# Top-k attention with a gated feed-forward layer: copies of near-limit columns by four tiles, and reciprocals transposed into another PSUM bank

## The chip, the cores and the metric

The kernel runs on one core of a Trainium2 chip. Its time is device microseconds of one execution; every kernel is run several times and the median counts. A profile is one further execution, recorded by the hardware profiler. Its engines are called by the names of the profile: PE is TensorE (matmuls; PEld are its weight loads), DVE is VectorE, ACT is ScalarE, POOL is GpSimd, SP is SyncE, which issues most DMAs here.

## The reference

For 8 batches, 8 heads, 576 rows and head width 64, attention keeps in each row the scores that are at least the row's 32nd largest, takes the softmax over them and multiplies by v. The heads side by side (512 columns) go through a feed-forward layer with a convolution of width 3 along the rows in its gate.

```python
scores = scale * np.matmul(q, k.transpose(0, 1, 3, 2))
kth = np.partition(scores, -32, axis=-1)[..., -32:-31]
scores = np.where(scores >= kth, scores, -1e9)
attn = np.exp(scores - np.max(scores, axis=-1, keepdims=True))
attn = attn / (np.sum(attn, axis=-1, keepdims=True) + 1e-09)
x = np.matmul(attn, v)                      # then heads side by side: (8, 576, 512)
h = np.maximum(x @ w_in, 0.0)               # 512 -> 1024
conv = conv_w[0] * h[s - 1] + conv_w[1] * h[s] + conv_w[2] * h[s + 1]
out = (h / (1.0 + np.exp(-conv))) @ w_out   # 1024 -> 512
```

## The kernel before

A tile is 128 rows of scores of one head (or the last 64 rows of both heads of a pair) by 576 columns; there are 288 tiles, 36 to a batch. A batch has two parts: first four pairs of heads with six tiles each, then the four pairs again with three tiles each, the last of which holds the 64 remaining rows of both heads (a "single" tile).

`iteration(it)` is a software pipeline written out by hand. In one iteration seven tiles are at work, each in another stage: TensorE computes the scores of tile it+3, ScalarE copies those of tile it+2 out of PSUM into one of eight row buffers (`rows`, 592 columns each, eight spare ones on either side of the 576 scores), VectorE takes the largest eight of each of seven chunks of tile it, and for tile it-1 the ranks near the 32nd out of these candidates (lines 281 to 288; the ranks are written into the spare columns of the tile's row buffer). For tile it-2 ScalarE computes signs against the estimated limit and counts them (`sides`), and GpSimd multiplies them in (`flip`). For tile it-3 ScalarE takes the exponential into a PSUM tile (`expo`, line 310). For tile it-4 VectorE finds the largest value below the limit (`below`), picks the limit (`select`, line 317) and multiplies mask and exponential with a running sum (`weigh`, line 331). For tile it-5 TensorE transposes the weights into bank `pt` (line 343) and ScalarE copies them out (`pT`, lines 348 and 351); with the tile's last head come the transposes of the 64 end columns into bank `mixed` (`tails`, line 356). One iteration later follows the product with v (line 375).

Within the loop the order of each engine's instructions is the order of this code for TensorE, ScalarE, VectorE and GpSimd; SyncE's and everything after the loop is ordered by a scheduler at build time. Matmuls of the feed-forward layer (lines 453 and 610) are put between the others by `run_units`, a fixed amount to an iteration as long as there are any ready.

Two steps beside this pipeline are touched by the change:

- `edges` keeps two spare columns of each tile (columns 6 and 7 of its row buffer, where the ranks next to the limit stand) for a count at the end of the kernel. It runs for eight tiles at once, on ScalarE (line 293), right behind the signs of the tile that fills the eighth row buffer. The first of the eight buffers is the next one that VectorE writes ranks into (line 285, the maximum of 56 candidates into columns 0 to 7), so that maximum waits for the copy.
- `norms` runs for each two pairs of heads, 32 times in all, in the iteration after VectorE has taken the reciprocals of the row sums (line 391). TensorE transposes the reciprocals (line 397), so far into bank `pt`, ScalarE copies them to SBUF (`rT`, line 399), and SyncE writes them to DRAM and reads them back spread over partitions (`rb`, lines 401 to 413), for GpSimd to multiply with (line 421).

The tiles `t_ps` and `e_ps` are parts of one PSUM tile, `weights_ps`, and so is `above`, which `select` reads. The bank `mixed` holds the end columns of the scores (columns 0 to 127), the transposed ends (128 to 255) and the product with v (256 to 511).

Of the kernel before, what the change touches and what calls it, by code (L numbers as in the profile page):

```python
# [29 lines left out]

XNB = 6
XBUFS = 8
EBUFS = 2
ZB = 3
SB = 2
# [33 lines left out]
def attend_and_feed(ctx: ExitStack, tc: tile.TileContext, q, k, v, weights, out, shared, finish=None):  # L69
    nc = tc.nc  # L70
    exact = finish is None
# [3 lines left out]
    ident, wi, wo, cw, cr, kth, edge = shared  # L75
# [31 lines left out]
    for i in range(10):  # L107
        nc.vector.memset(above[:, i:i + 1], float(S - 2 * (TOPK - (i + 1 if i < 8 else 0))))
    rows = const.tile([P, XBUFS, S + 16], F32, name="rows")
    sided = []  # L110
# [15 lines left out]
    def bank(name):  # L126
        return ps.tile([P, BANK], F32, name=name, tag=name, bufs=1)

    s_ps = [bank(f"s{h}") for h in range(2)]
# [113 lines left out]
    def evacuate(t):  # L243
        t.row = rows[:, t.n % XBUFS]
        x = t.x = t.row[:, 8:S + 8]
        at = TAIL if t.h else 0
        nc.scalar.copy(out=x[:, at:at + MAIN], in_=s_ps[t.h])  # L247
        if t.single:
            nc.scalar.copy(out=x[:, MAIN:S], in_=edge_ps[:, 0:TAIL])
        elif t.h == 0:  # L250
            r = t.n % XBUFS
            if r + 1 < XBUFS:
                first, step = r * (S + 16) + 8 + MAIN, S + 16 - MAIN
                ends = flat[:, first:first + 2 * step].rearrange("p (h c) -> p h c", h=2)[:, :, 0:TAIL]
                nc.scalar.copy(out=ends, in_=edge_ps.rearrange("p (h c) -> p h c", h=2))
            else:
                nc.scalar.copy(out=x[:, MAIN:S], in_=edge_ps[:, 0:TAIL])
                nc.scalar.copy(out=rows[:, 0, 8:8 + TAIL], in_=edge_ps[:, TAIL:2 * TAIL])
# [29 lines left out]
                    out=some, in_to_replace=m, in_values=some, imm_value=LOW)  # L288

    def edges(t):  # L290
        if t.n % XBUFS == XBUFS - 1 or t.n == NT - 1:
            n = t.n % XBUFS + 1
            nc.scalar.copy(out=edge[:, t.n + 1 - n:t.n + 1], in_=rows[:, 0:n, 6:8])  # L293

    def sides(t):
        t.cnt = att.tile([P, 1], F32, name="cnt", bufs=8)
        t.side = sided[t.n % SB]
        nc.scalar.activation(out=t.side[:, 2:S + 2], in_=t.x, func=AF.Sign, scale=-OVER, bias=t.row[:, 7:8],  # L298
                             accum_out=t.cnt)
# [6 lines left out]
    def expo(t):  # L306
        if t.h == 0:
            t.st.e2 = att.tile([P, 2 * S], F32, name="e2", bufs=EBUFS)
        t.e = t.st.e2[:, t.h * S:(t.h + 1) * S]
        nc.scalar.activation(out=e_ps, in_=t.x, func=AF.Exp, scale=scale, bias=t.shift)  # L310
# [79 lines left out]
        nc.vector.tensor_scalar(sums_ps[:, 0:n], pc.duo.sums[:, 0:n], 1e-9, None, ALU.add)  # L390
        nc.vector.reciprocal(rec[:, 0:n], sums_ps[:, 0:n])

    def norms(pc):
        n, w = pc.n, pc.c1 - pc.c0
        odd = pc.n % 2
        tp = bank("pt")
        nc.tensor.transpose(tp[0:2 * n, 0:P], pc.duo.rec[:, 0:2 * n], ident)
        rT = att.tile([SUMS, P], F32, name="rT", bufs=1)
        nc.scalar.copy(out=rT[0:2 * n], in_=tp[0:2 * n, 0:P])
        row = dram.tile([SUMS, P], F32, name="row", bufs=4)  # L400
        nc.sync.dma_start(out=row[0:2 * n], in_=rT[0:2 * n])
        rb = att.tile([P, 2, WIDE], F32, name="rb", bufs=1)
        for one in pc.duo.pcs:
            at = one.g % 2
            one.rb = rb[:, at, 0:w]
            for h in range(2):
                r = slice(h * D, (h + 1) * D)
                k, c = at * n + odd * lead // TAIL, odd * lead
                nc.sync.dma_start(out=rb[r, at, c:c + n // 2 * P].rearrange("d (i p) -> d i p", p=P),
                                  in_=row[k + h:k + n // 2 * 2:2, :].unsqueeze(0).broadcast_to([D, n // 2, P]))  # L410
                if odd:
                    k, c = (at * n, 0) if lead else (at * n + n - 1, w - TAIL)
                    nc.sync.dma_start(out=rb[r, at, c:c + TAIL],
                                      in_=row[k:k + 1, (1 - h) * TAIL:(2 - h) * TAIL].broadcast_to([D, TAIL]))
# [130 lines left out]
    class Contract:  # L545
# [11 lines left out]
        def split(self):  # L557
# [3 lines left out]
            if late and len(parts) == 1:  # L561
                for pool, name, n, size in ((att, "e2", EBUFS, 2 * S), (att, "pT", PTB, 2 * MAIN)):
                    for _ in range(n):
# [116 lines left out]
    pcs, work = [], []  # L680
    for b in range(B):
        for part, blocks in enumerate(PARTS):
            for g in range(NPAIR):
                pc = Box()
# [4 lines left out]
                for i in blocks:  # L689
# [4 lines left out]
                    for h in range(1 if single else 2):  # L694
                        t = Box()
# [5 lines left out]
    NT = len(work)  # L701
# [24 lines left out]
    def run_units(budget, only=None):  # L726
        while budget > 0.0 or (only is not None and only.cur is not None):
            for lane in lanes if only is None else (only,):
                if lane.cur is None:
                    lane.unit = lane.take()  # L730
                    if lane.unit is not None:
                        lane.cur, lane.left = lane.unit.pieces(), lane.unit.count
                if lane.cur is not None:
                    break
            else:
                return budget
            budget -= next(lane.cur)
            lane.left -= 1
            if lane.left == 0:
                next(lane.cur, None)  # L740
                lane.cur = None
                if lane.unit.final:
                    lane.finished.append(lane.unit)
        return budget
# [34 lines left out]
    av_next, out_next, rec_next, norm_wait, tail_next = [], [], [], [], []  # L779

    def iteration(it):
        nonlocal av_next, out_next, rec_next
        n = it + 3
        state.it = it
        pre, tA, tB, tC = (tiles.get(i) for i in (it + 2, it, it - 1, it - 2))
        tX, tD, tE = tiles.get(it - 3), tiles.get(it - 4), tiles.get(it - 5)
# [7 lines left out]
        crowded = n < NT and not work[n].single and work[n].h == 0  # L794
# [5 lines left out]
        if n < NT:  # L800
            t = tiles[n] = work[n]
            pc = t.pc
# [2 lines left out]

        if tC is not None and not exact:
            sides(tC)
            edges(tC)
        if pre is not None:
            evacuate(pre)  # L810
        if tE is not None:
# [31 lines left out]
        recs, rec_next = rec_next, []  # L843
# [6 lines left out]
        convert_act()  # L850
        if tX is not None:
            expo(tX)
        while tanh_now:
            e = tanh_now.popleft()
            e.tanh()
            if e.pooled():
                pool_tasks.append((it + 1, 2.01 * e.n / S + 0.1, e.gate_pool))
            else:
                gates.append(e)
# [3 lines left out]
        if norm_wait and norm_wait[0][0] <= it and not any(b < norm_wait[0][1].b - (norm_wait[0][1].g < XNB - NPAIR) for b in held):  # L863
            pc = norm_wait.pop(0)[1]
# [3 lines left out]
        feed = EARLY if state.blocks < BLOCKS else FEED if work[min(max(it, 0), NT - 1)].pc.part == 0 else LEAN  # L868
        state.credit = min(state.credit + (feed if it < NT + 5 else 9.0), PE_CAP)
        state.credit -= max(state.credit, 0.0) - run_units(max(state.credit, 0.0))  # L870
        for pc in recs:
            norms(pc)
        if both:
            tails(tE)
        if n + 1 < NT and not (work[n].single or work[n + 1].single or work[n + 1].h):
# [28 lines left out]
    with tc.manual_schedule(engines=engines) if engines else nullcontext():  # L904
        for pc in pcs[0:2]:
            fetch(pc)
        load_blocks(W_FIRST)
        for it in range(-3, NT + 6):
            iteration(it)
    if finish is not None:  # L910
        finish(edge_ps[0:1, 0:1])
    while expands or contracts or any(x.waiting for x in lanes) or pool_tasks or tanh_next or tanh_now or gates:
        it += 1
        iteration(it)
# [121 lines left out]
```

## Time and profile before

| | us |
|---|---|
| median of 3 runs (lowest, highest) | 1142.49 (1139.71, 1142.71) |
| profiled execution, its own time | 1140.73 |
| its span, first to last instruction | 1138.9 |
| first and last selection `weigh` (288 of them) | 28.0, 1068.5 |
| first and last of the 36 copies of line 293 | 47.8, 1063.2 |
| PE, DVE, ACT, POOL busy in the span | 1050.0, 1039.2, 988.1, 959.3 |

The loop over tiles takes nearly the whole span; until some 150 us the weights are converted beside it, and the last 70 us are the rest of the feed-forward layer. A busy time is the union of an engine's instructions as the profiler saw them. Matmuls are pipelined and their ends are modelled, so a busy PE need not be at its peak. A wait is an engine's idle time before an instruction, put down to the instruction of another engine that ended it; "issue" means that the profile shows no such instruction. Times in lists and rows are microseconds from the start of the span.

### The profile page before, as it was taken

The numbers are of one execution on the slowest core, as the hardware profiler recorded it, in microseconds if no ns is written. First come the engines' busy times: TensorE is split into PE (matmuls) and PEld (weight loads), VectorE is DVE, ScalarE is ACT, GpSimd is POOL, SyncE is SP. The second block draws the span as 40 slices with busy tenths as digits, with TensorE's granted clock in tenths as the row PEclk, the third lists the DMA queues.
The fourth block names the chain that finished last, engine by engine and source line by source line (L and its number), as shares of the span: only waits on it lengthen the run. The fifth ranks groups of instructions, "written<-read, shape, count | busy, mean of one in ns | idle before, by whom it ended". The sixth has DMA issues, their size and how long they took to land.

```text
span 1138.9 us, 27947 instructions
## 1 busy us (share of the span) xinstructions
PE 1050.0 (92%) x7970; PEld 769.6 (68%) x7970; DVE 1039.2 (91%) x5822; ACT 988.1 (87%) x2468; POOL 959.3 (84%) x1260
## 2 busy tenths in 40 slices
PE   5866689999999999999999999999899999999997
PEld 1443356676776767776777767776677767777785
DVE  6999999999899999999999999999999999999770
ACT  6999989898898888989999988989999888998651
POOL 5988978799898979899898979899898989899710
PEclk9988899999999999999999999999999999999999
DMA  7232221223221322223221222123222232132101
GB/s 254 85 102 79 78 85 55 61 79 107 70 79 51 109 87 73 63 75 127 60 79 62 95 86 87 53 87 117 67 61 82 70 111 87 50 90 71 32 25 50
DMA packets 71158, 92.28 MB, mean 81 GB/s; under 512 B 12848, under 2 KB 37712, under 8 KB 70992
## 3 DMA queue, kind: packets, MB, share of 16 engines
q1 hardware_dynamic: 70992, 90.38, 25.0%
q8 instruction: 66, 1.08, 0.4%
q14 instruction: 100, 0.82, 0.2%
HBM read 80.76 MB, written 9.58 MB: 79 GB/s over the span
## 4 chain that ended last, share of the span: by engine, by line
PE 59%; DVE 23%; ACT 14%; issue 2%; DMA 0%; POOL 0%; SPq 0%; ACTq 0%; DVEq 0%; POOLq 0%
PE mc L610 13%; PE me L453 12%; PE pt L343 9%; PE mixed L375 9%; PE s L241 7%; DVE cand L265 6%; DVE e L331 5%; DVE z L313 4%; ACT side L298 3%; ACT weights_ps L310 3%; PE mixed L378 2%; DVE cand L287 2%; PE mixed L224 2%; PE s L234 2%; PE weights_ps L610 1%
## 5 line engine op out<-in xcount | busy, mean ns | idle before, releaser
L265 DVE MAX8 cand<-rows 128x8 f32<-128x82 f32 (+1 forms) x2016 | 481.5, 240 | 0.0
L303 POOL TENSOR_TENSOR z<-rows,side 128x579 f32<-128x579 f32 x288 | 347.2, 1206 | 75.2 <-ACT side L298 74.1
L310 ACT ACTIVATE weights_ps<-rows,z 128x576 f32<-128x576 f32 x288 | 218.7, 760 | 26.5 <-DVE e L331 14.8
L331 DVE SCALAR_TENSOR_TENSOR e<-rows,kth,weights_ps 128x576 f32<-128x576 f32 x288 | 231.9, 805 | 0.9 <-PE mixed L356 0.7
L453 PE MATMUL me<-x_hi,wi 128*128 128x258 f32 (+1 forms) x952 | 229.6, 312 | 0.7 <-ACT g L467 0.7
L298 ACT ACTIVATE side<-rows 128x576 bf16<-128x576 f32 x288 | 222.3, 772 | 0.0
L313 DVE MAX8 z<-z 128x8 f32<-128x576 f32 x288 | 213.8, 742 | 0.0
L343 PEld LDWEIGHTS pt<-ident,e 128*128 128x128 f32 x1152 | 124.9, 144 | 125.9 <-issue 47.5
L610 PE MATMUL mc<-wo,split 128*128 128x512 f32 x732 | 197.4, 402 | 0.0
L343 PE MATMUL pt<-ident,e 128*128 128x128 f32 x1152 | 194.3, 293 | 3.0 <-DVE e L331 1.6
L351 ACT COPY pT<-pt 128x512 f32<-128x512 f32 x256 | 152.5, 596 | 44.2 <-PE pt L343 42.7
L241 PE MATMUL s<-k,q 64*128 64x512 f32 x512 | 180.7, 677 | 4.2 <-ACT rows L247 4.2
L247 ACT COPY rows<-s 128x512 f32<-128x512 f32 x288 | 166.6, 578 | 13.6 <-PE s L241 10.9
L375 PE MATMUL mixed<-pT,vn 128*64 128x128 f32 (+1 forms) x2560 | 168.1, 275 | 2.2 <-ACT pTt L361 2.2
L453 PEld LDWEIGHTS me<-x_hi,wi 128*128 128x128 f32 x952 | 162.7, 191 | 1.5 <-ACT g L467 1.4
L375 PEld LDWEIGHTS mixed<-pT,vn 128*64 128x64 f32 x2560 | 132.3, 141 | 24.3 <-issue 7.8
L610 PEld LDWEIGHTS mc<-wo,split 128*128 128x128 f32 x732 | 128.9, 189 | 20.9 <-POOL split L589 0.4
L453 PE MATMUL me<-x_lo,wi 128*128 128x258 f32 (+1 forms) x476 | 141.7, 298 | 0.0
L285 DVE MAX8 rows<-cand 128x8 f32<-128x21 f32 x576 | 105.9, 184 | 36.8 <-ACT edge L293 36.8
L486 POOL TENSOR_SCALAR t<-g,cr 128x256 f32<-128x256 f32 (+1 forms) x230 | 117.7, 512 | 0.0
L500 POOL TENSOR_TENSOR t<-t,t 128x256 f32<-128x256 f32 (+1 forms) x115 | 92.3, 803 | 9.6
L453 PEld LDWEIGHTS me<-x_lo,wi 128*128 128x128 f32 x476 | 90.9, 191 | 0.1
(133 smaller groups left out, 1778.1 us busy)
## 6 DMA issues: line engine op xcount, KB each, us to landing
k<-in_k_dram SPq DMA_DIRECT2D x64, 352.0 KB
q<-in_q_dram SPq DMA_DIRECT2D x64, 288.0 KB
vn<-in_v_main_dram SPq DMA_DIRECT2D x64, 256.0 KB
out_dram<-o SPq DMA_DIRECT2D x26, 256.0 KB
rb<-row SPq DMA_DIRECT2D x64, 96.0 KB
raw<-in_w_in_dram SPq DMA_DIRECT2D x16, 256.0 KB
vt<-in_v_tail_dram SPq DMA_DIRECT2D x64, 64.0 KB
raw<-in_w_out_dram SPq DMA_DIRECT2D x16, 256.0 KB
```

Of the source, the lines that this page charges most:

```text
L241: nc.tensor.matmul(s_ps[h], lhsT=qx[d, at], rhs=kx[d, h * TAIL:h * TAIL + MAIN], start=True, stop=True)
L247: nc.scalar.copy(out=x[:, at:at + MAIN], in_=s_ps[t.h])
L265: yield lambda c=c, at=at, n=n: nc.vector.max(out=t.cand[:, c:8 * CHUNKS:CHUNKS], in_=t.x[:, at:at + n])
L298: nc.scalar.activation(out=t.side[:, 2:S + 2], in_=t.x, func=AF.Sign, scale=-OVER, bias=t.row[:, 7:8], accum_out=t.cnt)
L303: nc.gpsimd.tensor_tensor(t.z[:, 8:S + 11], t.row[:, 6:S + 9], t.side, ALU.mult)
L310: nc.scalar.activation(out=e_ps, in_=t.x, func=AF.Exp, scale=scale, bias=t.shift)
L313: nc.vector.max(out=t.z[:, 0:8], in_=t.z[:, 10:S + 10])
L331: nc.vector.scalar_tensor_tensor(out=t.e, in0=t.x, scalar=kth[:, t.n:t.n + 1], in1=e_ps, op0=ALU.is_ge, op1=ALU.mult, accum_out=t.pc.sums[ ...
L343: nc.tensor.transpose(tp[:, i * P:(i + 1) * P], t.e[:, o + i * P:o + (i + 1) * P], ident)
L375: nc.tensor.matmul(a[r, 0:w], lhsT=st.pc.vn[:, h, i], rhs=st.pT[:, 1 - h if st.single else h, i, 0:w], start=(i == 0), stop=False)
L453: nc.tensor.matmul(mm[:, 0:w], lhsT=wt, rhs=xx, start=(n == 0), stop=(n == len(ops) - 1))
L610: nc.tensor.matmul(mm[0:m], lhsT=x[:, i], rhs=wo[:, e, f], start=start, stop=stop)
```

## The change

The copies of line 293 are made for four tiles at once instead of eight, 72 instead of 36 in all, and stand elsewhere: not behind the signs of the last of these tiles, but two iterations later, behind the exponential in the iteration in which that tile is weighed. The transposed reciprocals go into bank `s0` or `s1` of the main scores instead of `pt`; where the iteration's scores need both banks, the step would be put off by an iteration.

```diff
+EDGES = 4
     def edges(t):
-        if t.n % XBUFS == XBUFS - 1 or t.n == NT - 1:
-            n = t.n % XBUFS + 1
-            nc.scalar.copy(out=edge[:, t.n + 1 - n:t.n + 1], in_=rows[:, 0:n, 6:8])
+        if t.n % EDGES == EDGES - 1 or t.n == NT - 1:
+            n = t.n % EDGES + 1
+            at = t.n % XBUFS + 1
+            nc.scalar.copy(out=edge[:, t.n + 1 - n:t.n + 1], in_=rows[:, at - n:at, 6:8])
...
-    def norms(pc):
+    def norms(pc, tp):
         n, w = pc.n, pc.c1 - pc.c0
         odd = pc.n % 2
-        tp = bank("pt")
         nc.tensor.transpose(tp[0:2 * n, 0:P], pc.duo.rec[:, 0:2 * n], ident)
...
         if tC is not None and not exact:
             sides(tC)
-            edges(tC)
...
         if tX is not None:
             expo(tX)
+        if tD is not None and not exact:
+            edges(tD)
...
-        for pc in recs:
-            norms(pc)
+        while recs and not crowded:
+            norms(recs.pop(0), s_ps[1 if n < NT and work[n].single else 0])
+        rec_next = recs + rec_next
```

Line numbers shift by one to three in the changed kernel. On ScalarE, before, around the copy that ends with tile 87 (`rT` are reciprocals, `side` signs, `rows` the scores, `pT` and `pTt` transposed weights, `xt` a product with v, `weights_ps<-rows,z` the exponential, `weights_ps<-t` the gate):

```order
L310 ACTIVATE weights_ps<-rows,z 128x576
L514 ACTIVATE weights_ps<-t_5062,cw 128x256
L399 COPY rT<-pt 12x128
L467 ACTIVATE g_5070<-me 128x322
L298 ACTIVATE side_113,cnt<-rows 128x576
L293 COPY edge<-rows 128x16
L247 COPY rows<-s_122 128x512
L351 COPY pT<-pt 128x512
L361 COPY pTt<-mixed 128x128
L385 COPY xt_5089<-mixed 128x128
L310 ACTIVATE weights_ps<-rows,z 128x576
```

The same stretch of ScalarE in the changed kernel, from one iteration earlier; the copy in it holds tiles 80 to 83, and that of tiles 84 to 87 follows behind the fourth exponential after it:

```order
L312 ACTIVATE weights_ps<-rows,z 128x576
L295 COPY edge<-rows 128x8
L300 ACTIVATE side_109,cnt<-rows 128x576
L248 COPY rows<-s_121 128x512
L256 COPY rows<-mixed 128x2x64
L353 COPY pT<-pt 128x512
L312 ACTIVATE weights_ps<-rows,z 128x576
L515 ACTIVATE weights_ps<-t_5064,cw 128x256
L400 COPY rT<-s_121 12x128
L468 ACTIVATE g_5072<-me 128x322
L300 ACTIVATE side_113,cnt<-rows 128x576
L248 COPY rows<-s_122 128x512
```

So no copy of `edge` stands between signs and scores any more, and the copy of the reciprocals keeps its place. On TensorE, before, where the fifth set of reciprocals is transposed (what each waits for by semaphore in brackets):

```order
L453 MATMUL me<-x_hi,wi 128x322
L397 MATMUL pt<-ident,rec 12x128 [waits DVE_49,Activation_49]
L356 MATMUL mixed<-ident,e_2860 128x128
L224 MATMUL mixed<-k,q 128x128
L375 MATMUL mixed<-pT,vn 64x128 x8
L378 MATMUL mixed<-pTt,vt 64x128 x2
L343 MATMUL pt<-ident,e_2975 128x128 [waits DVE_49,Activation_49]
L241 MATMUL s_121<-k,q 128x512
```

The same place in the changed kernel:

```order
L454 MATMUL me<-x_hi,wi 128x322
L398 MATMUL s_121<-ident,rec 12x128 [waits DVE_49,Activation_49]
L358 MATMUL mixed<-ident,e_2861 128x128 [waits Activation_49]
L225 MATMUL mixed<-k,q 128x128
L377 MATMUL mixed<-pT,vn 64x128 x8
L380 MATMUL mixed<-pTt,vt 64x128 x2
L345 MATMUL pt<-ident,e_2976 128x128 [waits DVE_49,Activation_49]
L242 MATMUL s_121<-k,q 128x512 [waits Activation_49]
```

The order is the same; the transposes of the ends and the next scores each have a wait for ScalarE of their own now. VectorE and GpSimd keep their order up to the end of the loop.

## Rows read from the trace of the kernel before

**Rows 1.** Page, part 1: busy us, share of the span, instructions of each engine.
```profile
PE 1050.0 (92%) x7970; PEld 769.6 (68%) x7970; DVE 1039.2 (91%) x5822; ACT 988.1 (87%) x2468; POOL 959.3 (84%) x1260
```
**Rows 2.** By stage: PE, PEld, DVE, ACT, POOL busy us, clock, DMA share, GB/s.
```profile
177.00:1040.00 863.00, 837.32 (x6614) 623.39 (x6614) 818.88 (x4731) 779.35 (x1939) 772.08 (x995) 0.99 0.25 79
1062.00:1139.00 77.00, 66.65 (x413) 56.66 (x411) 36.87 (x81) 30.54 (x72) 19.78 (x31) 0.97 0.11 34
```
**Rows 3.** VectorE's waits over the span: us in total, times, longest us.
```profile
DVE rows L285 <- ACT edge L293: 36.8, 35, 1.9
DVE hot L317 <- ACT weights_ps L310: 7.8, 15, 1.3
DVE hot L317 <- ACT weights_ps L514: 3.5, 8, 1.0
```
**Rows 4.** ScalarE's waits over the span.
```profile
ACT pT L351 <- PE pt L343: 42.7, 68, 2.3
ACT weights_ps L310 <- DVE e L331: 14.8, 37, 0.7
ACT weights_ps L310 <- DVE rec L391: 7.7, 14, 1.1
```
**Rows 5.** Waits of TensorE over the span, and one of GpSimd.
```profile
PE mixed L356 <- ACT rows L255: 18.0, 8, 2.9
PE pt L397 <- ACT pT L348: 14.4, 8, 2.6
PE pt L397 <- ACT pT L351: 5.7, 7, 3.2
PE mixed L224 <- DMA q<-in_q_dram: 4.8, 1, 4.8
POOL xt L421 <- DMA rb<-row: 3.3, 2, 2.6
```
**Rows 6.** Timeline of 920.9 to 929.2 us: start, duration, instruction, idle before and what ended it.
```profile
920.92 0.19 ACT L293 COPY edge<-rows 128x16 f32<-128x16 f32 x1
921.01 0.57 ACT L247 COPY rows<-s 128x512 f32<-128x512 f32 x1
921.14 0.22 DVE L285 MAX8 rows<-cand 128x8 f32<-128x56 f32 x1 [1.15 <-ACT edge L293]
...
923.44 0.74 ACT L310 ACTIVATE weights_ps<-rows,z 128x576 f32<-128x576 f32 x1 [1.07 <-DVE rec L391]
...
926.39 0.27 ACT L255 COPY rows<-mixed 128x128 f32<-128x128 f32 x1
926.55 0.60 ACT L348 COPY pT<-pt 128x512 f32<-128x512 f32 x1
...
927.20 0.27 PE L397 MATMUL pt<-ident,rec 128*6 128x128 f32 x1 [2.58 <-ACT pT L348]
...
927.82 1.09 PE L375 MATMUL mixed<-pT,vn 128*64 128x128 f32 x16
927.86 0.25 ACT L399 COPY rT<-pt 6x128 f32<-6x128 f32 x1
...
929.07 0.33 PE L343 MATMUL pt<-ident,e 128*128 128x128 f32 x1
```
**Rows 7.** Line 293 over the span: ns min/median/max, first and last start us.
```profile
L293 ACT COPY edge<-rows x36: 186/189/249, 47.8 to 1063.2; 128x16 f32<-128x16 f32 x36
```
**Rows 8.** Line 331 over the span, as in rows 7.
```profile
L331 DVE SCALAR_TENSOR_TENSOR e<-rows,kth,weights_ps x288: 785/805/817, 28.0 to 1068.5; 128x576 f32<-128x576 f32 x144
```
**Rows 9.** Busy us in 281 to 285 us, columns as in rows 2.
```profile
281.00:285.00 4.00, 4.00 (x31) 3.49 (x31) 4.00 (x23) 2.01 (x6) 2.36 (x4) 0.57 0.03 10
```
**Rows 10.** Timeline of TensorE at 281.2 to 285 us.
```profile
281.49 1.98 PE L375 MATMUL mixed<-pT,vn 128*64 128x128 f32 x16
```
**Rows 11.** Waits in 279 to 290 us.
```profile
ACT pT L351 <- PE pt L343: 2.0, 1, 2.0
DVE hot L317 <- ACT weights_ps L310: 1.0, 1, 1.0
```

## The prediction

> **What bounds the kernel now.** I read the busy times first. Over the span TensorE, VectorE, ScalarE and GpSimd are all busy for 84 to 92% [rows 1], which names no bound. By stage it is clearer: in the 863 us of the steady loop VectorE is busy for 818.9 us (95%), TensorE for 837.3 (97%), ScalarE for 779.4 (90%), GpSimd for 772.1 (89%); the last 77 us belong to TensorE [rows 2]. A busy TensorE is partly a modelled one, so the waits come next. VectorE's largest by far is the one that the change is about: 36.8 us in 35 places, 1.05 us each, before line 285, ended by the copy of line 293 [rows 3]. Its other waits in the loop are the 7.8 and 3.5 us of line 317, which needs the bank of the exponential and the gate; TensorE holds it up for next to nothing.
>
> So VectorE is in front, and the copy of line 293 is where it waits for ScalarE. One such place, read in time order: the copy starts at 920.92 behind the signs, VectorE stands for 1.15 us and starts its maximum at 921.14, and what it does after that comes so much later; then ScalarE stands for 1.07 us until 923.44, since its next exponential overwrites what VectorE had still to read [rows 6]. The two engines wait for each other in turn: 36.8 us on the one side, 14.8 + 7.7 = 22.5 us before line 310 on the other [rows 3, 4]. ScalarE has a second partner: for transposes of TensorE it waits 42.7 us [rows 4], and TensorE waits for copies of ScalarE in its turn [rows 5]. This is the frame of the forecast: VectorE's wait can go, but the time gets shorter only as far as the pair of ScalarE and TensorE can follow.
>
> **The copies.** VectorE no longer waits there. The copy of tiles 8k to 8k+3 stands behind the exponential two iterations after the last of them had its signs; VectorE writes into the first of these row buffers again two iterations further on. An iteration is (1068.5 - 28.0) / 287 = 3.63 us, the copy 0.19 [rows 7, 8], so the data are some 5 us ahead of need, and the wait of 36.8 us is gone whole.
>
> What is late next is the exponential. If VectorE gains 1.05 us on ScalarE in every eighth iteration, ScalarE first uses up what it now stands waiting for VectorE, and from there VectorE stands before line 317, as it does now for 11.3 us. With ScalarE and TensorE as they are, they can shorten by those 22.5 us. Of 36.8 us, 36.8 - 22.5 = 14.3 come back as waits for the exponential. The bounds are wide: none comes back if TensorE and ScalarE work faster once they are pressed (gain 36.8), all of it if the pair has no reserve (gain 0). I take 22.5, since it is the only row that says how much ScalarE has to give.
>
> The copies themselves double, 36 more. One lasts 0.189 us, but the next instruction starts 0.09 us after it does (920.92 to 921.01) [rows 6, 7]. A copy half as wide is not in the trace; by these rows 36 cost ScalarE between 36 x 0.09 = 3.2 and 36 x 0.189 = 6.8 us. They come off what ScalarE can give. I take 3.6, near the start-to-start end, since copies run overlapped there too. Behind the exponential they also put the gate and the next signs back by 0.1 us; GpSimd and VectorE need these signs an iteration later.
>
> **The reciprocals.** Before, their transposes waited until ScalarE had copied the weights out of `pt`: 14.4 us in 8 places at single tiles and 5.7 in 7 others [rows 5]. Now they wait for the copy of the scores, which ScalarE makes earlier. But the next instruction on TensorE, the transposes of the ends (line 356), has a wait of its own now, for the copy of line 255, and that one starts only 0.16 us before the copy of the weights (926.39 and 926.55) [rows 6]. So TensorE gains the 0.6 us of line 348 in each of 15 places, 9 us of its 20.1, and it gains them mostly where it has no feed-forward work to do. Queued behind line 356 are the scores' end columns, the product with v and the next transposes, which ScalarE waits for.
>
> What line 356 waits for is a read of columns 0 to 127 of a bank in which it writes columns 128 to 255, and it costs 18.0 us in 8 places [rows 5]. The Trainium skill's page "PSUM — Partial Sum Buffer", section "PSUM bank collisions raise a hardware error", gives the reason: software is to guard the banks "by bank × quadrant", not by address. The trace agrees; by addresses alone the whole 20.1 us would go, by this rule the 9 us that I use.
>
> One more thing hangs on these stalls. After such a stall at 281 us, and after two others like it later, TensorE's granted clock fell: 0.57 in the mean over 281 to 285 us, that is mostly the lower level of 1.2 GHz [rows 9], and the sixteen matmuls of line 375 took 1.98 us instead of 1.09 [rows 6, 10]. ScalarE then waited 2.0 us for the transposes and VectorE 1.0 for the exponential [rows 11]. Three times 1.0 is 3 us if no such fall of this kind is left, and nothing if stalls shorter by 0.6 us still bring it; the stall of 2.58 at 927.20 had no fall behind it [rows 6], so I take half, 1.5 us.
>
> Costed at nothing: the copy `rT` keeps its place on ScalarE, so the way over DRAM to GpSimd starts when it did (GpSimd waits 3.3 us in two places for it [rows 5]). The next scores in bank `s0` must now wait for `rT`: it ends at 928.11, and TensorE's next transposes, which stand ahead of those scores, start at 929.07 [rows 6]; without this cover of a microsecond or more it would be up to 0.25 us in 32 places, 8 us. The step is never put off: with 12 tiles or 6 to two pairs of heads it always meets an iteration in which the new tile is a pair's second head. SyncE asks for some q and k a few requests later; TensorE waits for them once, at the start, 4.8 us [rows 5]. In the last stage TensorE's order changes, since the scheduler sets it; it idles 10.4 us of 77 there [rows 2], which bounds a gain, and I bound a loss by the same; value nothing.
>
> **The sum**, from the profiled execution's 1140.7 us: -36.8 + 14.3 + 3.6 - 1.5 = -20.4, that is **1120 us**. The median of the runs, 1142.5, is 1.8 above this execution; I leave that out as it is less than what separates the runs.
>
> **Rivals.**
>
> *VectorE bounds alone.* TensorE's busy time is modelled and ScalarE is busy for only 90%, so both follow: 1140.7 - 36.8 - 3 = 1101. For it: TensorE's waits and ScalarE's wait for one another are each larger than what they need to give. Against it: TensorE idles for only 863 - 837.3 = 25.7 us of the loop [rows 2]. The Trainium skill, "Perfetto Trace Analysis", section "Identifying the Most-Contended Engine", speaks for this one: it judges TensorE by its weight loads, here 623.4 of 863 us, 72%, and VectorE by its occupancy, so VectorE would be the engine to relieve and the whole wait would be won. The trace agrees as to who waits; that TensorE has this reserve no row shows.
>
> *TensorE and ScalarE bound.* Then the wait at line 293 only reappears at line 317, and the gain is what the transposed reciprocals give to TensorE, 9 us: 1132, or up to 1141 where even that lies in idle places. For it: TensorE 97% busy and ScalarE's 42.7 us of waiting for it. Against it: ScalarE's 22.5 us of waiting for VectorE would be left standing.
>
> *Slower.* ScalarE sets the pace once VectorE is ahead, and 36 more copies stand in its way between exponential and gate, 36 x 0.189 = 6.8 us, with nothing won elsewhere: 1147.5. It decides from the point where VectorE's waits at line 317 have grown by the whole 36.8 us.
>
> *The change does not do what it says:* the maximum of line 285 still has to wait for a copy, since one still stands before it on ScalarE. It would have to be 5 us late for that; the time would stay near 1141.
>
> **How the numbers follow.** I give the forecast (a gain of 12 to 30 us, 1111 to 1129) 0.57, VectorE alone (1100 to 1110) 0.17, TensorE and ScalarE (1130 to 1141) 0.18, slower 0.05, no effect 0.03. A difference under 0.3%, 3.4 us, can hardly be told from none. Faster is the first two and two thirds of the third: 0.86; the same, a third of the third and most of the last: 0.08; slower 0.06. The range for 8 in 10 takes in most of both neighbours: 1104 to 1136.
>
> **What would show it.** In the changed profile the row of VectorE waiting for `edge` should be missing; that of line 317 for the exponential should have grown from 11.3 to some 20 or 25 us; ScalarE's waits before the exponential should have shrunk to a few us; and TensorE's waits before the reciprocals should be short, with longer ones before the transposes of the ends. The forecast is wrong upward if the waits at line 317 reach 35 us or more, and wrong downward if they stay at 11 and TensorE's busy time in the loop falls with the time.

## The result, and the profile after

| | before | changed |
|---|---|---|
| median of 4 runs each (lowest, highest), us | 1142.45 (1139.71, 1142.71) | 1124.84 (1123.95, 1126.22) |
| profiled execution, us | 1140.73 | 1126.22 |
| its span | 1138.9 | 1124.3 |
| first to last selection (`weigh`) | 1040.5 | 1023.8 |
| rest of the span behind the last one | 69.6 | 71.8 |

The change takes off 17.6 us in the medians, a ratio of 0.985 (95% interval 0.983 to 0.987). 1120 was forecast, 4.8 lower; the time lies within the range given. The profiled execution is the slowest of the four, so its trace shows a gain of 14.6: 16.7 in the loop, less 2.2 behind it, and 0.1 ahead of it.

Part 1 of the page of the changed kernel answers to [rows 1]:

```profile
PE 1041.0 (93%) x7970; PEld 766.5 (68%) x7970; DVE 1044.5 (93%) x5822; ACT 985.1 (88%) x2504; POOL 959.8 (85%) x1260
```

The 36 more instructions on ScalarE are the copies. VectorE's busy time is 5.3 us longer than before, for as many instructions.

VectorE's waits in the changed kernel over the span (us in total, times, longest), against [rows 3]:

```profile
DVE hot L319 <- ACT weights_ps L515: 13.0, 25, 1.0
DVE hot L319 <- ACT weights_ps L312: 11.9, 21, 2.1
DVE z L315 <- POOL z L305: 1.8, 4, 0.6
DVE edge L959 <- ACT edge L295: 1.7, 1, 1.7
```

The row of 36.8 us, line 285 for the copy, has no successor. What is left of waiting for `edge` is the count at the end of the kernel, once. The pick of the limit (now line 319) waits 24.9 us for the bank of exponential and gate, against 11.3. For VectorE the loop adds up nearly: -36.8 + 13.6 + 1.8 (its wait for GpSimd before line 315) + 5.3 (busy) = -16.1, where the loop got shorter by 16.7.

ScalarE's waits, against [rows 4]:

```profile
ACT pT L353 <- PE pt L345: 48.0, 83, 2.0
ACT weights_ps L312 <- DVE e L333: 4.4, 10, 0.6
ACT weights_ps L312 <- DVE rec L393: 0.5, 2, 0.3
```

Of the 22.5 us that ScalarE stood before its exponential for VectorE, 4.9 are left; its waits for TensorE's transposes grew from 42.7 to 48.0. So VectorE, once the late one of the two, is now ahead of ScalarE, and ScalarE waits for TensorE instead.

TensorE's waits, against [rows 5]:

```profile
PE mixed L358 <- ACT rows L256: 19.9, 10, 2.9
PE mixed L358 <- ACT pTt L363: 8.3, 10, 1.8
PE s L398 <- ACT rows L248: 7.6, 7, 2.7
```

Before the reciprocals TensorE stood 20.1 us in 15 places, now 7.6 in 7. The transposes of the ends right behind them stand longer: 19.9 for the scores' end columns against 18.0, and 8.3 for the transposed end weights, where the trace of before has

```profile
PE mixed L356 <- ACT pTt L361: 2.7, 2, 1.8
```

Of the 12.5 us won before the reciprocals 7.5 are lost again one instruction later. The same reciprocals as in [rows 6], here 18 us earlier in the span, show how (start, duration, instruction, idle before and what ended it):

```profile
906.10 0.74 ACT L312 ACTIVATE weights_ps<-rows,z 128x576 f32<-128x576 f32 x1
...
909.21 0.27 PE L398 MATMUL s<-ident,rec 128*6 128x128 f32 x1 [0.86 <-ACT rows L248]
909.69 0.29 ACT L363 COPY pTt<-mixed 128x128 f32<-128x128 f32 x1
...
910.03 0.30 PE L358 MATMUL mixed<-ident,e 128*64 128x128 f32 x1 [0.55 <-ACT pTt L363]
```

The stall of 2.58 us before the reciprocals is now one of 0.86 and one of 0.55, and the exponential at 906.10, the one that had stood 1.07 us for VectorE (923.44 in [rows 6]), starts without a wait.

By stage, against [rows 2] (PE, PEld, DVE, ACT, POOL busy us, clock, DMA share, GB/s): the steady loop, the last 77 us, and four microseconds out of these.

```profile
177.00:1028.00 851.00, 833.91 (x6643) 622.31 (x6643) 826.61 (x4760) 780.92 (x1978) 776.01 (x1000) 1.00 0.26 81
1047.00:1124.00 77.00, 68.57 (x422) 59.57 (x421) 36.08 (x76) 28.61 (x67) 19.13 (x29) 0.95 0.10 32
1048.00:1052.00 4.00, 4.00 (x26) 3.83 (x23) 1.81 (x6) 1.81 (x6) 3.65 (x7) 0.57 0.03 7
```

TensorE is busy for 98% of the loop, VectorE for 97%. The granted clock holds at 1.00 from 177 to 1028 us: falls such as the one in [rows 9], of which the loop of before had three after 150 us (281, 411 and 670 us), are gone. One came at the end of the loop instead, behind a wait of TensorE of 1.79 us at 1046.85 for the copy of line 363. Behind the loop TensorE is busy for 1.7 us longer than before (63.1 against 61.3), most of the 2.2 us lost there; why is open, as the run of the copies alone (below) has the same fall and 70.0 us behind its loop.

### The profile page after: what moved, and what is told of

Read it like the earlier page. It is cut to its first block, busy times and chain, and to the rows that moved or that the text cites. A ratio compares the mean times of both kernels' runs of the same rounds, so it can differ in the third digit from the quotient of the medians.

```text
span 1124.3 us, 28000 instructions
## 1 busy us (share of the span) xinstructions
PE 1041.0 (93%) x7970; PEld 766.5 (68%) x7970; DVE 1044.5 (93%) x5822; ACT 985.1 (88%) x2504; POOL 959.8 (85%) x1260
## 4 chain that ended last, share of the span: by engine, by line
PE 72%; DVE 17%; ACT 8%; issue 1%; DMA 1%; SPq 0%; ACTq 0%
PE mc L611 15%; PE me L454 14%; PE pt L345 11%; PE mixed L377 11%; PE s L242 9%; DVE cand L266 4%; DVE e L333 3%; DVE z L315 3%; PE mixed L380 2%; PE s L235 2%; PE mixed L225 2%; ACT weights_ps L312 2%; PE mixed L358 2%; PE weights_ps L611 1%; ACT side L300 1%
## 5 line engine op out<-in xcount | busy, mean ns | idle before, releaser
L242 PE MATMUL s<-k,q 64*128 64x512 f32 x512 | 178.3, 671 | 3.7 <-ACT rows L248 3.6
L248 ACT COPY rows<-s 128x512 f32<-128x512 f32 x288 | 166.6, 578 | 16.2 <-PE s L242 13.2
```

The costliest lines, as they stand in the source:

```text
L242: nc.tensor.matmul(s_ps[h], lhsT=qx[d, at], rhs=kx[d, h * TAIL:h * TAIL + MAIN], start=True, stop=True)
```

## The experiments

Each is the changed kernel with one edit, unless it says before; every cut of code is shown against the changed kernel. Times are medians, ratios are to the kernel before run beside it (1140.2 to 1141.0 us).

**Each part alone: only the copies.** The reciprocals go into `pt` again.

```diff
-    def norms(pc, tp):
+    def norms(pc):
+        tp = bank("pt")
...
-        while recs and not crowded:
-            norms(recs.pop(0), s_ps[1 if n < NT and work[n].single else 0])
-        rec_next = recs + rec_next
+        for pc in recs:
+            norms(pc)
```

> The changed kernel with the reciprocals transposed into bank pt again, as before; only the copies by four are changed. Theory (the gain is VectorE's freed wait, of which somewhat more than a third comes back as waits for the exponential and the gate; the reciprocals give 1 to 3 us): 1126 to 1128 us, no wait of VectorE for a copy of edge, 24 to 28 us of waiting at the pick of the limit, TensorE's stalls before the reciprocals back at some 20 us. Rival (the two edits share the gain, since the stalls of TensorE for the reciprocals feed ScalarE's waits): 1131 to 1135 us.

1125.75 us (1124.31 to 1126.46), 0.986 (0.985 to 0.988). Its waits, VectorE's, TensorE's and ScalarE's:

```profile
DVE hot L319 <- ACT weights_ps L516: 13.4, 27, 1.0
DVE hot L319 <- ACT weights_ps L312: 12.3, 21, 2.5
PE pt L399 <- ACT pT L350: 9.8, 8, 1.5
PE pt L399 <- ACT pT L353: 4.6, 4, 3.3
PE mixed L358 <- ACT rows L256: 18.1, 10, 3.0
PE mixed L358 <- ACT pTt L363: 2.6, 2, 1.8
ACT weights_ps L312 <- DVE e L333: 4.4, 10, 0.6
```

25.7 us before the pick and 4.4 before the exponential: this is the changed kernel's picture without the reciprocals. All of the gain that can be told from nothing is the copies'. The stalls before the reciprocals shrank too, from 20.1 to 14.4 us, although the bank is the old one; I had expected some 20. Set against this run, the new bank takes 6.8 us from them (14.4 to 7.6) and adds 7.5 before line 358 (18.1 + 2.6 to 19.9 + 8.3): in sum TensorE gets nothing from it. This trace has no fall of the clock between 150 and 1030 us either. As far as one execution of each can tell, the new bank isn't needed for that.

**Only the bank of the reciprocals**, the copies as before; run twice, the second time for one profile.

```diff
-        if t.n % EDGES == EDGES - 1 or t.n == NT - 1:
-            n = t.n % EDGES + 1
-            at = t.n % XBUFS + 1
-            nc.scalar.copy(out=edge[:, t.n + 1 - n:t.n + 1], in_=rows[:, at - n:at, 6:8])
+        if t.n % XBUFS == XBUFS - 1 or t.n == NT - 1:
+            n = t.n % XBUFS + 1
+            nc.scalar.copy(out=edge[:, t.n + 1 - n:t.n + 1], in_=rows[:, 0:n, 6:8])
...
             sides(tC)
+            edges(tC)
...
-        if tD is not None and not exact:
-            edges(tD)
```

> The kernel before with the reciprocals in the bank of main scores; the copies stay by eight behind the signs. Theory: 1139 to 1142 us, VectorE still waits some 36 us for the copies of edge, TensorE's stall before the reciprocals under 8 us. Rival (the two edits share the gain): 1131 to 1135 us.

> The kernel before with the reciprocals in the bank of main scores, once more for its profile: of twelve executions the one profiled was the fastest (1137.8 us, the median 1144.3). Theory of its spread: which of TensorE's stalls are followed by a fall of the granted clock differs by execution; a time of 1143 to 1146 us then shows more such falls in the loop than the three of the first profile. Rival: the falls are as many, and waits of VectorE for the copies are longer by the difference.

The first: 1144.29 us, 12 runs from 1137.76 to 1147.48, 1.003 (1.002 to 1.004), above the 1139 to 1142 that I had expected; TensorE's stalls before the reciprocals come to 13.3 us, where I had expected under 8. The second: 1148.07. The runs of this kernel lie much wider apart than those of the others, and its two profiles are nearly its two ends, 1137.76 and 1148.07. First and second, VectorE's wait for the copy:

```profile
DVE rows L285 <- ACT edge L293: 33.8, 35, 1.9
```
```profile
DVE rows L285 <- ACT edge L293: 38.1, 35, 2.6
```

And one stretch of the loop, first and second (columns as above):

```profile
279.00:287.00 8.00, 8.00 (x85) 6.70 (x82) 7.57 (x49) 7.56 (x22) 5.77 (x8) 1.00 0.10 26
```
```profile
279.00:287.00 8.00, 6.07 (x46) 4.95 (x46) 7.40 (x45) 5.99 (x17) 5.26 (x7) 0.79 0.15 50
```

In the loop after 150 us the clock of the slower execution fell six times (282, 411, 551, 671, 801 and 930 us), that of the faster one three times (346, 408 and 664 us). So the theory holds that there are more falls, and the rival (as many) is out, though the wait for the copies is longer too. By the starts of the same selections in both, the slower one falls behind by 1.6, 1.1, 1.3 and 1.5 us at 282, 551, 801 and 930 us, where only it has a fall, together 5.5 of the 9.9 us by which its loop is longer; 2.8 were lost before 161 us. At the faster one's own fall at 346 us the distance doesn't change, so a fall need not cost anything. These are two executions of one kernel, so the order of the instructions alone doesn't set where the falls come. That the bank's change by itself makes the kernel 3 us slower is measured; which of its waits does so stays open.

**Where the copies stand.** Copies by four, but behind the signs as before.

```diff
             sides(tC)
+            edges(tC)
...
-        if tD is not None and not exact:
-            edges(tD)
```

> The changed kernel with the copies by four put back to the old place on ScalarE, right behind the signs of the fourth tile. Theory (what counts is that the next row buffers that VectorE writes belong to the other half, not the place): 1123 to 1127 us, the same as the changed kernel, no wait of VectorE for the copies. Rival (the place counts: a copy between signs and scores sets ScalarE back where TensorE and VectorE wait for it): 1130 us or more.

1125.65 us (1124.37 to 1126.46), 0.986 (0.985 to 0.988): the changed kernel's time. VectorE's waits:

```profile
DVE hot L319 <- ACT weights_ps L515: 14.5, 26, 1.4
DVE hot L319 <- ACT weights_ps L312: 13.6, 25, 2.5
```

VectorE has no wait for `edge` in the loop here either. It is the four tiles, not the place, that do it: VectorE's next row buffer is not among the four just copied, and it writes four other buffers before it comes to one of them again.

**What the copies cost.** No copies of `edge` at all, so the count at the end doesn't look at them.

```diff
-        if tD is not None and not exact:
-            edges(tD)
...
+    nc.gpsimd.memset(edge[:, :, 0:1], 1.0)
+    nc.gpsimd.memset(edge[:, :, 1:2], 1.1)
```

> The changed kernel without the copies of edge; the tile is filled once at the start, so the count at the end doesn't look at these columns. Theory (ScalarE and TensorE hold VectorE up, so ScalarE's work counts): 72 copies take 72 x 0.09 = 6.5 us to 72 x 0.2 = 14 us from ScalarE, 3 to 7 us of it on the time: 1118 to 1122 us. Rival (VectorE alone bounds): 1124 to 1126 us, no change.

1125.09 us (1121.91 to 1127.06), 0.986 (0.984 to 0.988). The 72 copies cost nothing that can be measured, so the theory missed; the rival has the right time, but its reason falls with the next experiment. The rows say where the freed time went:

```profile
ACT pT L353 <- PE pt L345: 50.4, 85, 2.1
DVE hot L319 <- ACT weights_ps L515: 14.8, 25, 2.0
DVE hot L319 <- ACT weights_ps L312: 12.2, 24, 1.8
```

ScalarE stands 2.4 us longer for TensorE, and VectorE no shorter for ScalarE.

**Who sets the pace of the changed kernel.** One kernel has less work for TensorE (of the three products with the split input of the feed-forward layer, that with the low part of x is left out, 512 of 7970 matmuls), one less for VectorE (the gate's product is left out in the loop, 99 instructions).

```diff
-            self.count = 3 * NCT
-            self.cost = self.count * (self.wide / 2400 + 0.003)
+            self.count = 2 * NCT
+            self.cost = 1.5 * self.count * (self.wide / 2400 + 0.003)
...
-                   for ct in range(NCT) for a, x in ((0, 0), (0, 1), (1, 0))]
+                   for ct in range(NCT) for a, x in ((0, 0), (1, 0))]
```
```diff
-            nc.vector.scalar_tensor_tensor(out=h, in0=self.to, scalar=1.0, in1=h, op0=ALU.add, op1=ALU.mult)
+            if state.it > NT + 4:
+                nc.vector.scalar_tensor_tensor(out=h, in0=self.to, scalar=1.0, in1=h, op0=ALU.add, op1=ALU.mult)
```

> The changed kernel without the products of the low part of x in the first matmul of the feed-forward layer (line 454), 512 of TensorE's matmuls, 424 of them in the steady loop at some 0.13 us each, 55 us; everything else is issued in the same iterations. Theory (TensorE sets the pace): VectorE's 25 us of waiting at the pick of the limit fall under 10, ScalarE's 48 us for the transposes under 30, and the loop from tile 40 to 279 gets 15 us or more shorter, 1095 to 1108 us in all. Rival (VectorE alone sets the pace): 1115 to 1122 us, only the last stage is shorter.

> The changed kernel without the product by the gate on VectorE within the loop (line 523), about 98 instructions of 0.46 us, which take 0.32 to 0.39 us from start to start, 35 us. Theory (TensorE sets the pace): 6 us or less are won, 1119 to 1125 us. Rival (VectorE alone sets the pace): 25 to 35 us are won, 1090 to 1100 us.

With less for TensorE 1100.18 us (1097.22 to 1101.96), 0.965 (0.964 to 0.967); with less for VectorE 1122.08 us (1121.45 to 1123.21), 0.984 (0.983 to 0.986). First and second, the waits that answer:

```profile
ACT pT L353 <- PE pt L345: 14.6, 31, 1.8
ACT weights_ps L312 <- DVE e L333: 13.3, 34, 0.6
ACT weights_ps L312 <- DVE rec L393: 7.6, 13, 0.9
DVE hot L319 <- ACT weights_ps L312: 4.8, 9, 1.6
DVE hot L319 <- ACT weights_ps L515: 2.6, 6, 0.8
```
```profile
DVE hot L319 <- ACT weights_ps L515: 23.4, 41, 1.1
DVE hot L319 <- ACT weights_ps L312: 22.4, 39, 2.2
ACT weights_ps L312 <- DVE e L333: 1.2, 4, 0.4
```

Taking work from TensorE wins 24.7 us (23 by the ratios), ScalarE's waits for it go from 48.0 to 14.6, and VectorE is pressed again: it stands 7.4 us before the pick. Taking 99 instructions of 0.44 us from VectorE wins 2.8 us (1 by the ratios, so hardly more than nothing), and its wait before the pick grows from 24.9 to 45.8: what it saves it waits. TensorE, with ScalarE between, sets the pace of the changed kernel.

**The same two in the kernel before.** The edits are those above.

> The kernel before with the same 512 matmuls left out. Theory (before the change VectorE's wait for the copies held up the loop, and TensorE took over only when that was gone): 10 us or less are won in the loop, some 6 in the last stage, 1125 to 1137 us, and the wait for the copies stays at 30 us or more; against the changed kernel with the same matmuls left out the copies then cost 25 to 35 us, most of the 36.8. Rival (TensorE sets the pace in both): both win the same, and the copies cost 15 to 18 us as they did.

> The kernel before without the product by the gate on VectorE within the loop (line 522), some 98 instructions or 35 us of VectorE. Theory (the copy is late because ScalarE is, and ScalarE is late because of TensorE and, behind each wait of VectorE, because of VectorE; VectorE's own work sets the pace in few iterations): 10 us or less are won, 1130 to 1140 us, and VectorE's wait for the copies grows to 45 us or more. Rival (VectorE alone sets the pace before the change): 25 to 35 us are won, 1105 to 1116 us, and the wait for the copies stays.

With less for TensorE 1113.65 us (1110.34 to 1114.91), 0.976 (0.974 to 0.978); with less for VectorE 1130.04 us (1128.66 to 1134.69), 0.992 (0.990 to 0.994). The first and the second:

```profile
ACT weights_ps L310 <- DVE e L331: 25.8, 67, 0.7
ACT weights_ps L310 <- DVE rec L391: 8.5, 11, 1.1
DVE rows L285 <- ACT edge L293: 24.0, 31, 1.7
```
```profile
DVE rows L285 <- ACT edge L293: 42.8, 35, 2.2
DVE hot L317 <- ACT weights_ps L310: 13.1, 21, 1.2
DVE hot L317 <- ACT weights_ps L514: 9.1, 17, 1.0
ACT weights_ps L310 <- DVE e L331: 8.6, 25, 0.9
ACT weights_ps L310 <- DVE rec L391: 4.1, 6, 0.8
```

I had thought that VectorE, being late before, would leave TensorE's relief little to win. It won 26.5 us, and between the selections of tiles 40 and 279 21.3, as in the changed kernel (838.7 to 817.6, 21.1). VectorE's relief won 10.8 us, where the changed kernel gives 2.8. So neither engine alone set the pace of the kernel before: both reliefs show in the time, and the whole change is still worth 13.5 us (1113.65 against 1100.18) with TensorE relieved, and 8.0 (1130.04 against 1122.08) with VectorE relieved. With less for TensorE the copy wait itself shrank from 36.8 to 24.0 us: a third of it went with TensorE's work, though neither VectorE's work nor the copies had changed.

These two pairs also test the rule of the prediction, that the change wins what ScalarE stood waiting for VectorE before its exponential. With less for TensorE these waits go from 25.8 + 8.5 = 34.3 us to 13.3 + 7.6 = 20.9, 13.4 less, and the time is 13.5 shorter. With less for VectorE they go from 12.7 to 1.2, 11.5 less, and the time is 8.0 shorter. VectorE's wait for the copies, 24.0 and 42.8 us, would have said otherwise in both.

**Two waits taken on in the changed kernel.** VectorE's 24.9 us are for a bank in which ScalarE writes exponential and gate and VectorE reads constants, `above`. In one kernel these constants lie in SBUF; in the other ScalarE copies the scores ahead of the signs.

```diff
-    above, sums_ps = weights_ps[:, 2 * BANK - 32:2 * BANK - 22], weights_ps[:, 2 * BANK - 16:2 * BANK - 16 + SUMS]
+    above = const.tile([P, 10], F32, name="above")
+    sums_ps = weights_ps[:, 2 * BANK - 16:2 * BANK - 16 + SUMS]
```
```diff
-        if tC is not None and not exact:
-            sides(tC)
...
+        if tC is not None and not exact:
+            sides(tC)
```

> The changed kernel with the ten constants that the pick of the limit compares with (tile above) in SBUF and no longer in the PSUM tile of the exponential and the gate, so that VectorE's 25 us of waiting for these two can't occur there. Theory (TensorE sets the pace of the loop; VectorE's wait at the pick is only where it shows): the wait goes away, others grow, 1121 to 1126 us. Rival (VectorE alone sets the pace): the 25 us are won, 1100 to 1106 us.

> The changed kernel with ScalarE copying the scores out of PSUM ahead of the signs in each iteration instead of behind them, to give TensorE its banks 0.76 us earlier. Theory (TensorE sets the pace and waits for copies of scores and of end columns): its waits before lines 242, 358 and 398 shrink, 3 to 8 us are won, 1117 to 1122 us. Rival (the signs, and GpSimd's product with them, are then late): exponentials wait for GpSimd, 1126 us or more.

Constants in SBUF: 1184.72 us (1182.83 to 1189.82), 1.041 (1.038 to 1.043). The pick, changed kernel and this one (busy us in total, mean ns | idle before):

```profile
L319 DVE SCALAR_TENSOR_TENSOR hot<-weights_ps,cnt,z 128x10 f32<-128x10 f32 x288 | 62.4, 217 | 25.7 <-ACT weights_ps L515 13.0 <-ACT weights_ps L312 11.9
```
```profile
L320 DVE SCALAR_TENSOR_TENSOR hot<-above,cnt,z 128x10 f32<-128x10 f32 x288 | 142.3, 494 | 0.1
```

The wait is gone, but the instruction itself lasts 277 ns longer in the mean, 80 us over 288 of them. So the run doesn't tell what the wait for the bank is worth; it put a larger cost in its place (the last section).

Scores ahead of signs: 1140.80 us (1140.09 to 1143.94), 1.000 (0.999 to 1.001), 16 us worse than the changed kernel.

```profile
ACT rows L248 <- PE s L242: 52.6, 69, 2.1
ACT pT L353 <- PE pt L345: 19.1, 44, 2.1
DVE hot L319 <- ACT weights_ps L515: 19.9, 37, 1.8
DVE hot L319 <- ACT weights_ps L312: 17.2, 29, 1.6
```

ScalarE now stands for TensorE's scores, 52.6 us against 13.2 in the changed kernel, ahead of signs that could have run meanwhile. That is the time that the rival had, but not its way: exponentials wait 1.1 us for GpSimd. Its waits for transposes fall by 28.9, so it stands 10.5 us more in the two together, and VectorE waits 12.2 us more. No version that does the whole work and is faster than the changed kernel came out of these.

## Why the prediction was right, step by step

- *The wait of 36.8 us goes whole.* Right: its row is missing, also with the copies at the old place. The reason given, data ready some 5 us ahead, is not needed for it; the other half of the row buffers is enough.
- *14.3 us come back before the pick, from ScalarE's 22.5 us of waiting for VectorE.* Right, and the term that carries the number: 13.6 came back, and of the 22.5 us 17.6 went, 4.9 stayed. The time fell by 16.7 in the loop and by 17.6 in the medians. The rule under it, that an engine pair can shorten by the time the follower stood for the leader, gave 22.5 and so held to 5 or 6 us here. That 13.6 lies so near 14.3 is in part luck: the loop kept 16.7 of the 36.8 us, so some 20 came back, and the pick has only 13.6 of them; 5.3 came back as longer instructions and 1.8 as a wait for GpSimd, which the sum didn't have.
- *The copies cost 3.6 us.* Wrong: nothing measurable. ScalarE stood 48.0 us for TensorE in the same loop, and the copies' time comes off that. The cover was there in [rows 4], as 42.7 us; I had counted ScalarE as having nothing to spare beside the 22.5.
- *The reciprocals give 1.5 us by the clock.* Wrong as far as the runs show. The falls in the loop did go, but with the copies alone too; on one chip the copies alone came to 1125.75 and both parts, with the copies at the old place, to 1125.65; and the bank alone makes the kernel before 3 us slower. That a fall costs something was right: at 281 us the kernel before falls 1.6 us behind the first run of the bank alone, which has none there. So a part of the 16.7 us is the clock's, and came with the copies; the runs don't separate how much. As to the stalls it was right that line 358 waits next, with 7.5 of 12.5 us coming back there; but the 9 us that TensorE was to gain were the wrong size, as against the copies alone it gains none. The Trainium skill, "PSUM — Partial Sum Buffer", section "PSUM bank collisions raise a hardware error", wants a bank guarded as a whole or by quadrant, not by address; the trace agrees, with 19.9 us before line 358, which writes other columns than those that line 256 reads.
- *Not in the sum:* VectorE's busy time, 5.3 us more in thin slices (2.4 of it in the maxima over chunks, 242 ns each instead of 240), 1.8 us of waits for GpSimd before line 315, and the 2.2 us behind the loop. The two terms of VectorE's wait came to -36.8 + 13.6 = -23.2, where the sum had -22.5; these three give 9.3 back, where the copies and the clock in the sum had given 2.1. That is how the trace comes to -14.6 (-13.9 by these terms) and the forecast to -20.4.

The rival in which VectorE alone bounds (1101) is out: 24.9 us stand before the pick, and less work for VectorE wins 2.8 us at most. That TensorE and ScalarE leave no reserve (1132 to 1141) is out too, as the pick's wait stayed far below 35 us. But the frame, VectorE in front until the pair takes over, was too simple. With TensorE relieved in the kernel before, the loop got shorter by as much as in the changed one: the waits of three engines for each other add up, and the 36.8 us were in part TensorE's already. The forecast came out near since it took the gain from a row of waits of the follower, not from who was in front, and by luck in the rest, as two terms that no run shows (3.6 back for the copies, 1.5 won by the reciprocals) took the place of a part of the 9.3 that the sum lacked.

## What to carry to other kernels

Where two engines wait for each other in turn, look at what the other one stands waiting in return before pricing a wait by its own size. In the three pairs of kernels here, freeing VectorE's waits of 36.8, 24.0 and 42.8 us won 17.6, 13.5 and 8.0 us, and ScalarE's waits in return shrank by 17.6, 13.4 and 11.5. To free such a wait it was enough that the reader works on another half of the buffers than the writer needs next; 36 more small copies on an engine that waits elsewhere cost nothing that could be measured. Before taking a second wait away, take some work from one engine at a time and see which relief shows in the time.

## What the runs showed of the hardware that was not expected

The pick of the limit is a VectorE instruction on 128x10 values. With one input in PSUM it lasts 217 ns in the mean; with all in SBUF 494, up to 1264, and the kernel gets slower by 5%. In the timeline of that kernel the long ones lie beside GpSimd's product of signs and scores:

```profile
573.57 1.26 DVE L320 SCALAR_TENSOR_TENSOR hot<-above,cnt,z 128x10 f32<-128x10 f32 x1
573.57 1.23 POOL L306 TENSOR_TENSOR z<-rows,side 128x579 f32<-128x579 f32 x1 [2.98 <-ACT side L301]
```

They start and end within 0.03 us of each other, as if VectorE's instruction could only finish with GpSimd's. So it is throughout: each of the 120 picks that last over 450 ns ends within 0.03 us of the end of a GpSimd instruction, and the 27 during which GpSimd has none last 211 ns in the mean. The Trainium skill, "SBUF — State Buffer", section "Who interferes with whom", says that a VectorE instruction with two inputs in SBUF contends with a GpSimd instruction that reads SBUF, and calls what they share an exclusive lock; the trace agrees. Ten constants a partition in PSUM cost 25 us of waits for their bank and save 80 us of this.

The granted clock fell in one execution of a kernel at places where it held in another. Four such falls cost 1.1 to 1.6 us each, and a fifth, at 346 us, nothing. In the changed kernel six stalls of 0.8 to 0.9 us before the reciprocals (the one at 909.21 is the last) were not followed by a fall, and those of 2.68 us at 78.70 and 1.79 us at 1046.85 were. In the kernel before, stalls of 1.93 us and of 2.59 (twice) were, and that of 2.58 at 927.20 was not: the length of a stall alone doesn't decide.
